# Batches 3 and 4 of a gated-linear-attention and mixer kernel: q and k transposed by 24 transfers that ScalarE issues

## The chip, the cores and the metric

The kernel runs on one core of one Trainium2 chip. The metric is device time in microseconds (us), the median of several runs; lower is better. A profile of one execution goes with it. Engines are named as in the profile: PE is TensorE's matmul (PEld its weight loads), DVE is VectorE, ACT is ScalarE, POOL is GpSimd, SP is SyncE, which only issues transfers. SPq is SP's own instruction queue.

## The reference: what is computed

q, k, v and alpha have the shape 4 batches x 8 heads x 768 positions x 48. Two parts follow each other. The first is a recurrence over positions with a state of 48 x 48 per head; the second is a mixer over the positions and channels of what the first gives (384 channels, a low-rank position mixing of rank 32, and a two-layer MLP of width 1536).

```python
for t in range(S):
    state = alpha[:, :, t, :, None] * state + np.einsum('bhd,bhe->bhde', k[:, :, t], v[:, :, t])
    y[:, :, t] = np.einsum('bhd,bhde->bhe', q[:, :, t], state)
...
h = xt @ U @ V                       # xt: x with positions last
u = x + h.transpose(0, 2, 1)
ch = np.maximum(u @ w_ch1, 0.0) @ w_ch2
return (u + ch).astype(np.float32)
```

Inputs and the output are 32-bit floats; the kernel works in bfloat16 with 32-bit accumulation.

## The kernel before, in words

**Chunks.** The recurrence is done in chunks of 128 positions, six per batch (c = 0 to 5). Batches are numbered from 0, so the third and fourth batch are 2 and 3. In batch 0 all chunks, and in batch 1 the first four, go through `stage_pair`, which works on halves of 64 positions; the other two of batch 1 and all of batches 2 and 3 go through `stage_gla`, which the change touches. For one chunk `stage_gla` does this, in names used below:

- ACT takes the logarithm of alpha into `lt` (line 525); a matmul with a triangle of ones sums it up over the chunk (lines 532 and 534); ACT takes the exponentials of plus and minus that sum, `aa` and `ai` (lines 542, 543), and of the totals, `tot` (line 545).
- POOL (or DVE) multiplies: `rk` = k times `ai`, `rq` = q times `aa` (line 552, both). v is cast to `rv`.
- `rk` and `rq` are transposed into `kT` and `qT` (tiles kt and qt): the head dimension comes to the partitions. In batches 0 to 2 PE does it, four 128 x 128 transposes each against an identity (`f_tr`, line 565), and DVE or ACT copies the result out of PSUM (`f_ev`). In batch 3 SP issues one transposing transfer for each (line 576), SBUF to SBUF, 128 x 512 bfloat16.
- Scores are matmuls of kT and qT (`f_sc`, line 590, eight per chunk), masked by DVE into `pm` (line 600). The state is a matmul of rk and rv (line 613), added to the state before it on DVE (line 640) and scaled on POOL or DVE (line 624). The chunk's output is the matmuls of line 652 (from the state) and of line 657 (from pm and rv), copied to `xb`.

The pools of these tiles are small: three of kT, four of qT, three of rq and four of rk, so a transpose into a kT also waits for the scores of the chunk that had that tile before.

**Mixer.** `stage_mix` does the low-rank part and adds it to x (lines 672, 702 and 703), and transposes the sum with PE (line 723). `mlp1` is 24 entries per batch of three 384-wide matmuls each (line 754), each followed by a ReLU out of PSUM on ACT (line 764) or DVE (line 766). `mlp2` is, per chunk, twelve 384-wide matmuls in three groups of four (line 780), then an addition on DVE (line 786) and one or two output transfers by SP (lines 789 and 791).

**Order.** Nothing is ordered by loops at run time. Every operation is entered in a plan with a list of the engines it may use and an estimate of its cost in ns. The estimates serve an offline search only. What runs is the string TABLE: three characters an entry, two of them the operation's number (base 64) and the third the engine, P, A, D, G or S. An entry that begins with ++ issues as many filler matmuls (line 259) as its third character's number says. SLOTS gives, in order of first use, which buffer of its pool each tile takes. So each engine runs its entries in the order of TABLE, and an instruction at the head of an engine's queue that waits for a semaphore holds all that follow it on that engine.

Batches overlap in the order: the chunk work of batch b + 1 lies between the `mlp1` and `mlp2` matmuls of batch b, so that PE has work while other engines prepare chunks. PSUM has eight banks, shared by all of this. Inputs go into 36 buffers (`io`), so a load also waits for a buffer.

In the order before, the engines hold, of the entries that the change's steps touch:

| | before |
|---|---|
| transposes of batches 2 and 3 | batch 2: 12 groups on PE with 12 copies out (6 ACT, 6 DVE); batch 3: 12 transfers on SP |
| ReLU entries on ACT, batches 0 to 3 | 17, 13, 12, 12 |
| ReLU entries on DVE, batches 0 to 3 | 7, 11, 12, 12 |
| filler matmuls | 9, near the start |

Of the kernel before, what the change touches and what calls it, by code (L numbers as in the profile page):

```python
# [15 lines left out]
TABLE = """
++EA8SCcACePChABQSETAEVPA+SCgACjDClPBASCzAC1PCfA++BA9SCiDCkPBISCnADjAA-SCdGCrPCsDBDSC3AC4ACmACoPCpD++DBBSC2AC5DDlPDnAABS
AFGAGPCqDBCSC6GC0GC8PC+DEWAEXADmABMSD8ABLSDkGC7P++BC9DDCPDDDCtPC-PDADDBDBKSDqGCuDBESDKAEYAD+PDEPDFDDoAAHDDMPDOADNABFSDQD
BJSDpGDPABHSDLGBRSEZGBSSBYSCvPCwPCxDDZPDGPDsPDuABUSDHPDJADrPDtDBGSDRGDSPEaDDyPBNSBTSEUGDzPD0DEBAD-ADIAECGBOSEAAEDGDvPDwD
DUAEcPEbPEdDDaPDbDD1PD2DAJPEeAEfPEhDEgDG2AGfAGhPDTPDVDDcPDdDBPSD9GCyAAKABVSGiAGlGBgSAOSAPGBWSGjAGmGBcSAgSAhGAASADGBXSG4P  # L20
ALGAMSGgGANGBoSAQSARGBZSAiSGkAG7AG5AG8GDxDBaSG6AG9GASSBbSAeSEiPEjPBkSBiSAWSDWPDXDBdSD3PD4PAUSBfSBeSEEPEGAD5PD6AAaSAcSBhS
A2SAmSAYSEFPEHAEkDDePElPEmPELPDfPBlSBqSEnPEpAHmADYDDgPEoADhADiDEMPBjSBpSEOPENDEIPEKDEJDGnPHoPAoSBmSAqSAkSEPPGoPGqDHNAHPP
EQPESDERDGpAGrPGsDGtDD7AHpAHQAEqPErPEwPE5PE2PHqAHrAGuPHRAGvDGwDEsAEtPE6PE7AExPE3PE4DE8PFBPFCDEuPEyAE9PE+AAwSB0SAuSAySEzP
FJPFFPFGDFKDE0PIVAEvAE1AGyPE-PFlPFmAG+PFADFjPFkAFHPFIDBnSG-PHBDFnPFoDGxGFPPAsSACSA6SBrSHSAHAAHCPG3GHFPHGDHHDHEDGzPA4SAfA
AjGFdPFeAG1DA0SF3PF1PF2DHDDF4DH-AHIGG0AF5PIBPIFAFhPFiAIXPHJPF6AIEAFfPFgAIYAFQAHTDBsSBtSFNPAXGHtGHvPAVGATGFVPFtPFWAIDAHxD
FODFTPFUAHUGHWPIZAHKPHLAFuDHOGHcPHYAHdDFrPAdGHsGFDPFEDHVPHXDHuPHeGHfDICAHwDFsAAnAFLPFMAHMAHgDHiPFRPFSAHZPHaDHbDB8SBvSB3S
HyPB4SBwSHzDIGDH0DAZGAbGFZPH6PFaAFXPFYAA3AFxPHhPFvPFwAIbGIdPIfDFbPFcAHjPHlAHkDHnGH1PH2DH3DIaGFzPF0AH4DB2SIIPIKDIHGIJPIcP
IeDH7PFpPILAFqDH8PH9DH+AIgPH5DFyDIMPIODCASINDIhDArGApGAIGAlGGTPF7PGZPK0AK2PGBPAvGBuSAzAIAAIPPIRDIQDAtAITPK4AAxGGUPGaPF8P
IiDIWAISGIjPA7AK5AGCPK3AIUDAEGK6AIkAIlPA1AImAA5GGDPF9PGEDI1PI2DIpPIqDInPGNPIvPIwDItPIoDIuDGVPGWDIzPI0DF+DBySBxSGASF-SGOP
KLAKNPKPAKTGKOAKSGBzSIrPIsAIxPIyDGPPI3PI4DGbPGcDKfAJNPJdPI9PJHPKhPJOALeAJIDJFPJeAJGDI+AKiAI5PKjALJALzAI6DJTPJUDI7PI8AKQA  # L30
LgPJVPLjAKRALiAKlALkAJLPJMDJRPLhAJJPJDPJnPJKDJjPKUPB1SJWAJSAJPPI-PJAAKkAJoDJkDGQDJBPJCAJZPCCSJaAKWAK7DK9PK-DGFSKMGKbPKcD
JhPJiAKgGKmGKnGKvPL1PL2AJEAB-SJXPLLPLNALMAJQDLPAKwDK8DJfPJgDKoPKpPKrAB+SKqAGYSK+PLOAGdSB6SGXSB9SLlGLADJYDKxDL3AL5GCESJlP
JmAJbPGeSB5SLQGCBSL4GKVPKXDJvPK1AKsPKtDCFSJcAB7SCISCRSCMSLBPKYPLDDJwPNlANnPNpAL7PL9ANrANoALCDGGSGHPKuDLEPLFDKZDJxPJyDLGD
KyPKzAGIPL6PL8DLHPGJPKaDCQSNqALIDLnPLpDGKDGSSCUSJ0SCDSCGSCHSLSPLRGLTPKBPGRSLmGLoPLKALZPLqDKCPLaDLrPLtDLsDLfALUALVALWPLYD
L+PKDPKEDJ7POKAOMPLbGLxPNsGNuSNtGNvSOdAOfPOhAOjAOgAOOAL-DMADLXDJ8PJpPLuPLvDLwDJ9PJ+DJqPKdPKeDN3AN5PN6AOPAOwAOiAL0GMBPMCD
N7ALyAONAJ1PNmGNzPGLSJzSN0DCJSN+GCOSOSGCSSOlGGMSCYSCTSCWSKFSCKSOkGOmSCLSJrPLcPLdAJ2PN9ANwPNxDMDPJsDNyDMEAKGPCVSMTPOnSMLP
MNPMODOQAN8AMFPKHPMHPMRPJ3PN1PMMDMPPMQAMIDN4GMGDMJPMKDOyPO2AOzAO1AKIPMjPMtPMuAMUDMSDMVPMWDMkAPDAKJDMlPMbPMnPMoAMxPPFPPGA
J4DMmDMvPMfPMwDMgDMcAOASNDPNEAM5PM6DMXPMyDMZPMaDN2DMdPO0AO4DM3PCNSMrPMsDMpPMqACZSMeDCPSN-GOBSCaSO6SNBPOoPMYDOqDM7PNCAM1P
MhPM9PM2AMiDOpDO3GO5SCXSOUSORGOTSM-POeGOLGOFPOGDOHDPHAM4ANMPNHPOYPMzPM+DM8DOZDOrPNRPNFPNGAOaGNAAOsDNIPOuPOvDNNPOCPODDO7P
PIGPKSPJGPLSJ6SCbSM0ANJPNbPNSPJ5SOxGO+POEDOIPOJAJtSO9DOtDJuSNOPO8DPBPO-DPADPCAOVPOWDOXDNcPPEANWPPMPPODPNDNTPNUDNVSObPOcA  # L40
NgPPPPPQANhPPRPPSANiPNKDKKSNLSKASPTPPUDPZPPbPPcDPVPPWDNXPPaDPfPPgDNdPPhPPiDPXPPYAPdPPeDNYPPjPNjDP7PP8APpPNeDPqDPrPPkDNPD
NQSPlPPxPPsDP1PPtPPuDPyDQDPQHPQNPQOAQBPQCDQLPQMAQIAPnPPoAP-PQAAPzPP9PPmDP0AQRPQTPQUDQSDNZDNaSNkSQEDQPPQVPQQAP+AJ-SNfSQFP
QGAQJPPvPPwDQuPQaPP5PP6AQKAP3PP4DQzPQfPQWPQ0PP2DQXPQYDQZSQ1PQ2DQ3SQgPQbPQkPQcPQdDQeSQhPQvPQiDQjSQlPQwPQpPQxDQySQmPQnDQoS
QqPQrPQsDQtS
"""
SLOTS = """
AAAABBBCAACDCDAEAEFAAGAFGAHBBAACAIBBECFJBBDBCAAKBLCABHCBDABMCNCCHDBBBOCPDAQDRASTEDAAGCCUBFCVACBDWXEGCBABYCCFBCAHDBCDFDHD
AABAGAZAaBDbcdABefgEhBijABDACCDBACEFFGIJDHBHGALKNCCMPQORSBBBEDFCGTVCUXHABFCGCWYZaDECBFBGBAABAEDHCCCGACAAAABCAcbdeGDHAECB
AHADfGDCBghjBAAFCDHBBBGiCBADHCCFDEGHACADEDCECABAEBBCDECABAEBGDCCDBBBBFGEDCBFGACJIADBHGEDBAACGDCBAACABLGACDFCCADBGDFBCCAC
HBEFHADABABCDAAGBABBEDGFBBECNKCFCBBAPDBBADAECDBABBHCEBCABCBDHCCDEBBCFECDQHBCECSBBGCCBBAECAECCMDGBABBCBAHBRAFVUDAAAAOEBTA  # L50
XCHDFDADAYZWabGCEHBBBAACDBCGACBDACDAGdECDcefgACFBBDAHBBGEABBAACBFDAHAECGBCABCCBAACABFABCDBACBAEFABCDHAjChCiBADIBABJGCDFC
HBAGCDDHBCEAFBHCBAEDCHAADCDFAHDGAACFAHACFAHCAEHADEFBCPAFBAADHFCDCKBBBACEHBCBGFEBAHCDBBEDHBAECABDQBADHCDEABADADHEABADAEDB
BCAEFDCFDAECAFBDDEBABFDCGEDBEDBGAEBDBEDAGHCEACBADCDEBA
"""


# [81 lines left out]
def kernel(  # L138
# [383 lines left out]
    def stage_gla(b, c, sprev, xb):  # L522
# [51 lines left out]
        if (b, c) in QUEUE_T:
            for dst, src in ((kT, rk), (qT, rq)):
                P.add({"SP": 900.0}, lambda e, dst=dst, src=src: nc.sync.dma_start_transpose(dst(), src().rearrange("t h w -> t (h w)")), r=[src], w=[dst], kind="T")
# [268 lines left out]
```

## Time and profile before

| | |
|---|---|
| median of three runs | 165.25 us (163.98 to 166.45) |
| the profiled execution's own time | 166.14 us |
| its span, first to last instruction | 164.4 us |
| mean granted TensorE clock | 0.990 |
| line 754 (mlp1 matmuls), 288 | 52.0 us busy |
| line 780 (mlp2 matmuls), 300 | 54.2 us busy |
| line 565 (PE transposes of rk and rq), 64 | 5.8 us busy (219 ns each, pipelined) |
| line 576 (transposing transfers on SP), 12 | 2.5 us from issue to landing for kt, 3.2 for qt |
| loads of q, k, v, alpha, 96 of 192 KB | 3.6 to 3.9 us from issue to landing |

Busy time is the time in which an engine had at least one instruction under way; matmuls overlap in the pipeline, so the mean duration of one is longer than what it adds. What one matmul adds is read from the chain, where a group's time is the step to the next group. Transfers are issued by a sequencer (SPq rows) and moved by 16 shared DMA engines, whose mean busy share is given by stretch. "Idle before, releaser" names what an engine last waited for.

### The profile page before, as it was taken

Reading aid. Unit: us, or ns where it says so; the run is one execution under the profiler, and the core shown is the slowest. Engines: PE = TensorE matmul, PEld = TensorE weight load, DVE = VectorE, ACT = ScalarE, POOL = GpSimd, SP = SyncE. Lnnn points to the kernel's source line nnn. Section 1 sums busy time; section 2 is a strip of 40 time slices with the busy share of each in tenths; the row PEclk is TensorE's granted clock in tenths of the full one; section 3 lists DMA queues with packets and bytes.
Section 4 is the critical chain, followed back from the end, with each engine's and each line's share of the span. In section 5 each row is a group of like instructions: output and inputs, shape, how many; then the busy total and the mean of one; then the engine's idle time right before and its main releaser. Section 6 shows DMA issues by size and latency. Waiting matters only on the chain.

```text
span 164.4 us, 4606 instructions
## 1 busy us (share of the span) xinstructions
PE 153.7 (94%) x1767; PEld 101.2 (62%) x1767; DVE 118.6 (72%) x254; ACT 86.5 (53%) x223; POOL 60.7 (37%) x99
## 2 busy tenths in 40 slices
PE   5875999999998999999999979999999999999992
...
DMA  5999999999999999899998759889653550105053
GB/s 136 291 312 305 273 264 222 311 260 287 238 273 290 231 212 197 172 220 208 214 196 174 145 114 227 193 160 183 114 106 68 136 175 4 48 0 168 5 186 102
DMA packets 94758, 30.49 MB, mean 185 GB/s; under 512 B 88432, under 2 KB 94704, under 8 KB 94736
## 3 DMA queue, kind: packets, MB, share of 16 engines
...
q14 instruction: 8, 0.07, 0.1%
...
## 4 chain that ended last, share of the span: by engine, by line
PE 76%; SPq 11%; DVE 4%; DMA 3%; POOL 2%; issue 1%; ACT 1%; DVEq 0%; POOLq 0%
PE ps L780 27%; PE ps L754 27%; SPq L325 10%; PE ps L702 2%; PE ps L590 2%; PE ps L565 2%; PE ps L723 2%; PE ps L402 2%; DMA io<-in_moe_w_ch_dram 2%; DVE pm L437 2%; PE ps L657 1%; PE ps L509 1%; DMA out_dram<-ou 1%; PE ps L532 1%; PE ps L652 1%
## 5 line engine op out<-in xcount | busy, mean ns | idle before, releaser
L780 PE MATMUL ps<-w_sb,h1t 128*128 128x384 bf16 (+2 forms) x300 | 54.2, 320 | 0.9 <-ACT tot L545 0.9
L754 PE MATMUL ps<-uT,w_sb 128*128 128x384 bf16 x288 | 52.0, 326 | 0.0
L764 ACT ACTIVATE h1t<-ps 128x384 bf16<-128x384 f32 x54 | 25.5, 501 | 25.0 <-PE ps L754 24.8
L780 PEld LDWEIGHTS <-h1t 128*128 128x128 bf16 x300 | 26.7, 97 | 16.3 <-issue 1.9
L754 PEld LDWEIGHTS <-w_sb 128*128 128x128 bf16 x288 | 26.6, 98 | 15.5
L766 DVE TENSOR_SCALAR h1t<-ps 128x384 bf16<-128x384 f32 x42 | 22.2, 553 | 12.3 <-PE ps L754 11.6
L600 DVE TENSOR_TENSOR pm<-ps,maskc 128x512 bf16<-128x512 f32 x28 | 18.1, 684 | 3.4 <-PE ps L590 2.5
L786 DVE TENSOR_TENSOR ou<-ub,ps 128x384 f32<-128x384 bf16 (+2 forms) x25 | 13.2, 534 | 9.1 <-PE ps L780 8.2
L552 POOL TENSOR_TENSOR rq<-io,aa 128x384 bf16<-128x384 f32 x12 | 10.9, 916 | 12.3 <-DMA io<-in_q_dram 7.7
L552 POOL TENSOR_TENSOR rk<-io,ai 128x384 bf16<-128x384 f32 x12 | 10.9, 916 | 11.3 <-DMA io<-in_k_dram 5.8
L703 DVE TENSOR_TENSOR ub<-xb,ps 128x384 bf16<-128x384 bf16 x24 | 12.0, 550 | 2.3 <-PE ps L702 2.1
L437 DVE TENSOR_TENSOR pm<-ps,maskp 128x512 bf16<-128x512 f32 x20 | 13.1, 683 | 0.6 <-PE ps L426 0.2
L270 POOL CAST rv<-io 128x384 bf16<-128x384 f32 x18 | 9.1, 511 | 11.9 <-DMA io<-in_v_dram 11.9
L266 ACT CAST xb<-ps 128x192 bf16<-128x192 f32 (+1 forms) x21 | 8.0, 388 | 8.0 <-PE ps L657 7.3
L543 ACT ACTIVATE aa<-ps 128x384 bf16<-128x384 f32 x14 | 7.0, 497 | 8.5 <-PE ps L534 8.5
L270 POOL CAST w_sb<-io 128x384 bf16<-128x384 f32 x17 | 8.8, 533 | 0.9 <-DMA io<-in_moe_w_ch_dram 0.9
L385 POOL TENSOR_TENSOR rq<-io,aa 128x384 bf16<-128x384 f32 x8 | 7.6, 950 | 3.3 <-DMA io<-in_q_dram 1.9
L624 POOL TENSOR_TENSOR st<-sm,tot 128x384 bf16<-128x384 f32 x3 | 2.5, 830 | 15.3 <-DVE sm L640 15.3
L542 ACT ACTIVATE ai<-ps 128x384 bf16<-128x384 f32 x14 | 7.0, 503 | 1.8 <-PE ps L534 1.7
L379 ACT ACTIVATE aa<-ps 128x384 bf16<-128x384 f32 x10 | 5.0, 506 | 5.4 <-PE ps L371 5.4
L525 ACT ACTIVATE lt<-io 128x384 bf16<-128x384 f32 x14 | 7.2, 532 | 0.0
L385 DVE TENSOR_TENSOR rk<-io,ai 128x384 bf16<-128x384 f32 x4 | 6.2, 1554 | 1.1 <-ACT ai L378 1.1
...
## 6 DMA issues: line engine op xcount, KB each, us to landing
...
```

The source lines that it names most:

```text
L270: nc.gpsimd.tensor_copy(dst, src)
L325: lambda e: nc.sync.dma_start(t().rearrange("p (h j) d -> p h (j d)", j=2), src[b, hs, sl, :].rearrange("h (p j) d -> p h (j d)", j=2)),
L385: eng.tensor_tensor(jh(dst()[:, :, 0:D]), raw(a), jh(x()), op=ALU.mult)
L437: nc.vector.tensor_tensor(dst, s2, maskp.to_broadcast([C, 2, 2, C]), op=ALU.mult)
L552: eng.tensor_tensor(dst()[:, :, 0:D], a(), x(), op=ALU.mult)
L600: nc.vector.tensor_tensor(pm()[:, :, par, :], s2, maskc.to_broadcast([C, HP, C]), op=ALU.mult)
L703: P.add({"DVE": 465}, lambda e, c=c, hb=hb: nc.vector.tensor_tensor(ub()[:, c, :], xb()[:, c, :], hb()[:, 0:DM], op=ALU.add), r=[hb] + xk( ...
L754: nc.tensor.matmul(hb()[:, 0:TW], lhsT=w1_sb[:, ct, jt * 128 : (jt + 1) * 128], rhs=u_half(uT, ct, tt, b in QUEUE_U), start=(ct == 0), sto ...
L764: nc.scalar.activation(dst, hb()[:, 0:TW], AF.Relu)
L766: nc.vector.tensor_scalar_max(dst, hb()[:, 0:TW], 0.0)
L780: nc.tensor.matmul(hb()[:, 0 : hi - lo], lhsT=h1()[:, jt, c * C : (c + 1) * C], rhs=w2_sb[:, jt, lo:hi], start=(jt == 0), stop=(jt == NJ - 1),
L786: P.add({"DVE": 468}, lambda e, hb=hb, lo=lo, hi=hi: nc.vector.tensor_tensor(ou()[:, lo:hi], ub()[:, c, lo:hi], hb()[:, 0 : hi - lo], op=A ...
```

## The change

Batch 2's chunks too are transposed by transfers, and all 24 transfers of batches 2 and 3 are issued by ScalarE on its own queue instead of by SP. TABLE and SLOTS are replaced as a whole. All else is the same, the estimates of other operations included.

```diff
     PAIRS = {0: 3, 1: 2, 2: 0, 3: 0}
-    QUEUE_T = tuple((3, c) for c in range(6))
+    QUEUE_T = tuple((b, c) for b in (2, 3) for c in range(6))
     LAST, CUT = 3, 240
...
         if (b, c) in QUEUE_T:
             for dst, src in ((kT, rk), (qT, rq)):
-                P.add({"SP": 900.0}, lambda e, dst=dst, src=src: nc.sync.dma_start_transpose(dst(), src().rearrange("t h w -> t (h w)")), r=[src], w=[dst], kind="T")
+                P.add({"ACT": 1200.0}, lambda e, dst=dst, src=src: nc.scalar.dma_start_transpose(dst(), src().rearrange("t h w -> t (h w)")), r=[src], w=[dst], kind="T")
         else:
```

The new TABLE has 1068 operations where the old one has 1080. Read entry by entry, with the operations numbered in the order in which the code enters them:

| | before | after |
|---|---|---|
| transposing transfers | 12 on SP (batch 3) | 24 on ACT (12 each for batches 2 and 3) |
| transposes on PE, batch 2 | 12 groups, 12 copies out | none |
| ReLU entries on ACT, batches 0 to 3 | 17, 13, 12, 12 | 14, 3, 7, 13 |
| ReLU entries on DVE, batches 0 to 3 | 7, 11, 12, 12 | 10, 21, 17, 11 |
| products and casts on POOL, batches 2 and 3 | 29 | 33 |
| filler matmuls | 9 | 2 |

In the new order ACT issues batch 2's transfers among the mlp1 and mlp2 matmuls of batch 1, chunks in the order 0, 2, 1, 5, 3, 4, and batch 3's among those of batch 2, chunks in the order 0, 3, 1, 4, 2, 5.

More of the change, by code (lines that the diff above doesn't have):

```diff
@@ L21 @@
[L21 to L35, printed above, removed]
@@ new lines @@
+CtPClPBESDKADMPEYABRSEZDDFDCnACoPBISC9DC-PCuDCqDCpDDGPDBDBMSDPADjAD8AD+PDOADNADlPDoADADDmAABSAFGAGPDnAAJPAKDBGSDRGBJSDpG
+BHSDLGBFSDQDBKSDqDEbPEdAAHAAIGBSSEaGBLSDkGBYSCvPCwPCxACyADrPDtADZPDTPDVDDHPDaPDbDBUSD-ABNSECGBPSDIADsPDuADJADSPDUDDcPDdD
+EcPEeDG2AGfAEBADvPDxDDwDDyPDzPD0DDWPDXDEAABOSEDGBTSEUGGhPGjAD9ABWSGmGGiABgSBcSBVSGkABXSGgGAASG4PG6AELPADGBaSG9GAgSAhGAeS
+AfGAiSDYDD4PD1PD2DBZSASSD3PEEPEGDAjGEMPENDD5PG5AG8GAMSANGG7AAOSEfPEgDEhDDfPD7AD6ABiSEFPAPGAQSBbSARGAUSAVGBeSBdSEHADePElP
+EiPAWSAXGBhSHmABoSDgPDhAAaSBjSAcSHNADiABkSEjPAYSBfSBqSAoSBmSEkDEIPEKDGlDBlSHoPHqAHtGHrABpSAqSAmSAuSAkSAsSBnSAwSEJDAySA0S
@@ new lines @@
+A6SB0SEmPGoPGqAEPPBrSEnPEoAA2SA4SACSEOPHpAEpAHPPHRAHQAHSAHUGGnPGpDEQPESDERDGuPGvDEqPGrPGtDGsDGwDAdGBuSAbGErPEsABwSE8PE2P
+EzPEwPE9PE+ABsSE3PE4DGxDExPFDPEtPB8SB4SFJPEyAE0PE1AEuPEvDE5PFBPFCDFHPFEDG-PHBAE6PE7AGyPFIDFhPFiAG+PATAHAAFfPFgDE-PFFPFKD
+FADF3PF4AF1PF2DHCPHDDFGDB1SBtSBvSFdPHEDF5PFlPFmDFeDFnPGzPG3AHFPF6AHsDHGDHTDHHDHIGFNPFOAFLPFoAFjPFkDFMAFrPFsAG0AIVAFpPFVP
+HvPHuPHxDHwAHWPHYDFTPFUAFqDG1DIXPIYAHyPHzDH0DFRPIZAFtPFuDH-AHVPHJPHXDIBPIFAICAFSAAZGFzPF0DFxPFyDIEAIDAFvPFwAFWDHKPHLAHMA
+HOGHcPHdDHeDHnGH1PH2DHfDHZPHbDHaDIbGIdPFZPFaAIfAFPPFQAIHGIJPFbPFcAIGGIIPIKDAnAFXPFYAArAILDIaGIcPIeDHhPHiPH3GH4DH5DH6PH7P
@@ new lines @@
+HjPHkAH8PH+AAxAApGIMPINDIODIgPIhDAlGF7PGNPGBPGZPHlDIiDHgGIAGITPIPPIQDIRDISDAvGAzAAtAGaPGTPGCPGUPA7GA1AH9AKwAKyPKzAK1AIUA
+IWGIjPA5GIkDF8PA3GGDPGEDGGSALGAEGIlPImAK2AF9PF+DF-SGASK0AIpPIqDIvPKdAKLABxSItPIuDIwDGVPIzPCASKfPKhAKgAKjAKNPCESKPAKTGInP
+IoDB2SBzSBySGbPKiAGWDCBSCCSB3SB+SIxPIyAKOAI0DKSGI1PI2DGOPIrPIsDGcDGPPB6SB5SI3PI4DB7SB9SGYSGFSJJPJLPI5PI6DJRPJjPJSDJKDJnP
+JoDJlPJmDGXSCGSI9PGQDGRSCFSJMDJfPCMSGSSCQSB-SCISCDSKQALWALYPCHSGeSK3GLDAKVAKUAJkAGdSK5ALaAKRAI+AJPPJQAKWPKXDJHPJIDJFPJGD
+JgDJDPLpALrPLcAJNPJODKYDJXPJYDGHPKMGKZPKaDLFPJTPJUDJBPI7PJCDI8DLbAKkGKmAJhPJiDJEDJbPK4GI-PJADJZPJaDKeGKrPKsDLsAK6AJcDLZA
@@ new lines @@
+GIPJvPKbPKcDLtAKlGKnAKoPKpDKqDLuGNZALGALHAK7PK8DK9DKtDJwPGJPNbPJpPKuPKvDKxGK+PK-DJxPJyDJ0SJzSJVPJWDCUSCRSGKDGMSGLSLwACVS
+CSSCKSCYSLJAJdPJeDCJSCLSCWSCNSCOSCTSLvGLxALIACaSCPSLBPLyPLzDL0DKBPJqPLKGLMALeGLgACZSLADLCDLEGLRPKCPLSDJ7PKDPKEDKFSLLGLNA
+LOPLdGLfALhPLiDLjDNcANgGNeANdAN+ANiANfANhGNjAJ8PLXGLkPJ1PLTGLnPLlDLmGORALoALqAOAPOBAODAOTPOXAOWAOUAOYGJrPL1PLPDLQDLUPOVA
+OZGL2DOCAJ2PNkPLVDL3PNlDNmDNaAJ9PJ+DJ-SKASCXSL4AL-PMBPMCDMADL7PKGPOEAMHPL5PL6DMFPKHPL8DJsDJuSNrANpPNqDOkAMDPMEDL9PL+AJ3P
+NnPNtPNvANuANxAOmPOnAMGDMRPMVPMWANoDJ4DJ6SJtSMTPCbSOrGMhPMIDMJPMKDMUDMXPMSAMbPMcDMYDOaAMnPNyGMiAMPPOoANwAObAOqAO3AOpAMQA
@@ new lines @@
+MfPNzDMoDN1AMtPMuDMrPMNPMODMgDMpPMLPMqDMMDMZPO5PO7AMdPO6AMaAM3PM4DMvPMwDMsDMeDMlPOcPOeDM5PM6DMmDMxPN0AOFGOsGNsGN5POSGN6D
+N7DMjPMkDNAPOtAOGGOuAMyAOHAM7POIAJ5SN-GOMPONDNBPMzPM0DOdDNCPOfPNFPNDDNESOOGOiPOjAOgDM8PO9GO-AOvPOxDOwDN2PN3DN4DNPPKIPOJP
+OKDKJDO8GO+ANGPM9PNQPN8PN9AOlGOhDOyPOzDO0GNHPPAPNUPO1PO2AOLDOPPOQAPBDM1PO4GPCDPDPPEANVPM2APFPPGANWPNXDPPPPHPPIDPJPPNPNRP
+NKPPKDPTPPQDPVPNLPPLPPODPRPNMPPMAPWDPUDPXPPYAPSDPbPPpPPdPPqAQDPNSDQEDPeAQHPPfPQFPQGAPcAM+DM-SPzPP0DPgDQIDP-PPhPQADPxPPZP
+PyDPiDP7PPvPPrPNTSPlPPmAP5PNIDP6APjPPkDP3PPaAP4DNYSNJSKKSQBPQCAPnPQTPP1PPtPNNDPwAPsANOSPoAP2DQJPP9PP+AQiPQKPP8DQUPPuAQLP
@@ L45 @@
+QMDQNSQnPQjPQOPQVPQWDQXSQoPQPPQYPQpPQqDQrSQkPQlDQmSQQPQRDQSSQZPQdPQaPQbDQcSQePQfPQgDQhS
 """
 SLOTS = """
[L47 to L50, printed above, removed]
@@ new lines @@
+AECBJFEDGAFACHBAGCACDFBAGBAHOEFCBADDGBACBFCEFBABCDFAAABGEADFCACBBGHBEDCDFABGCADABEEFBACBABGADHCEDDACBCAGACHCBDAEBBGFACAE
+BBGHADFCDBAAHAHBBBGBEABGHDKCCCCGIAAHLMQCPRNSEBACHCDUVFWYDEHBCBFHTCBaDXcdZeBCFbBABBCABHACGECBBDHGEDDAHAGDAAAGBDACCBAABFDC
+BCCBABDCCCCGABDBAECAAGfgCBhiBjBADECJFHADAOHCFCGCABBGCBEBABCCCFACHEBADCBBBAAAGDDHAAADECAGBBBHACABCFHGBCDKACFCGHEAFACCABAC
+GBCBADABGFABCBLCDFEGAFABABCADCDGECFGACBBBDFGCACDFCDAEEABDBABBCADADGAEFBBAGBCBECAAFBGCECDABABCFAACHAFEBCCHFBAEHACFAHCEFAC
+HEFBCCGEFBCDFHCEGDHFBBHFCBHFCAGDACHBEDCAGB
```

19 lines of the change are left out of this document (3 added, 16 removed).

## The prediction

> **What bounds the kernel now.** I read the page first (busy shares, slices, chain), then the table of stretches, then the rows of the transposes that already run as transfers, then the chain of waits around them.
>
> ```profile
> PE 153.7 (94%) x1767; PEld 101.2 (62%) x1767; DVE 118.6 (72%) x254; ACT 86.5 (53%) x223; POOL 60.7 (37%) x99
> ...
> DMA  5999999999999999899998759889653550105053
> ...
> PE 76%; SPq 11%; DVE 4%; DMA 3%; POOL 2%; issue 1%; ACT 1%; DVEq 0%; POOLq 0%
> ```
>
> TensorE is busy 94% of the span and is 76% of the chain that ended last; SP's issue of the first loads is the other part.
>
> ```profile
> 34.00:54.00 20.00, 19.41 (x289) 12.86 (x288) 17.29 (x39) 15.11 (x41) 14.22 (x24) 1.00 1.02 271
> ...
> 64.00:82.00 18.00, 18.00 (x163) 12.10 (x162) 12.99 (x27) 13.54 (x37) 5.41 (x7) 1.00 0.96 202
> 82.00:92.00 10.00, 10.00 (x145) 7.14 (x144) 9.02 (x19) 6.68 (x17) 5.37 (x7) 1.00 0.91 184
> 92.00:100.00 8.00, 7.09 (x92) 4.92 (x91) 6.35 (x12) 4.17 (x12) 2.77 (x5) 1.00 0.63 131
> 100.00:115.00 15.00, 15.00 (x137) 9.39 (x134) 11.14 (x23) 6.50 (x18) 7.49 (x10) 1.00 0.92 191
> 115.00:135.00 20.00, 19.91 (x215) 12.44 (x214) 15.05 (x29) 6.26 (x14) 3.09 (x5) 1.00 0.54 123
> ```
>
> Columns: stretch, its length, then busy time of TensorE, weight loads, VectorE, ScalarE, GpSimd, then granted clock, DMA share, GB/s. From 34 us on TensorE idles only 0.59 + 0.91 + 0.09 = 1.6 us before the tail. So a microsecond taken off TensorE there is a microsecond off the end, if nothing else becomes late. VectorE (9.02 of 10 us at 82 to 92) is next, DMA is near full until 92 us, ScalarE has room.
>
> ```profile
> L576 SPq DMA_TRANSPOSE kt<-rk x6: 1191/1218/1308, 92.8 to 123.8; - x6
> ...
> DMA to landing us min/median/max: 2.4/2.5/2.6
> ```
>
> ```profile
> L576 SPq DMA_TRANSPOSE qt<-rq x6: 1188/1388/1719, 94.3 to 125.1; - x6
> ```
>
> ```profile
> 94.58 0.85 SPq L576
> 95.44 0.05 issue
> 95.49 1.94 DMA out_dram<-ou
> 97.44 0.25 ACT tot L545
> ```
>
> A transpose holds its issuing sequencer 1.19 to 1.72 us; ten that stand alone in SP's rows have a mean of 1.36. It lands 2.4 to 4.1 us after its issue begins. The last fence is the chain: the one TensorE stall of 0.91 us runs through SP's transposes.
>
> **TensorE's part, removed.** Batch 2 loses 12 groups of four transposes. The chain's rows give 0.22 us for a group ("PE ps L565 x4"), 0.67 us for three. 12 x 0.22 = 2.64 us, all in stretches where TensorE is 100% busy (64 to 92 us): on the path. The 12 evictions go too: on ScalarE 6 x 0.6 = 3.6 us, on VectorE 6 x 0.42 = 2.5 us, both beside TensorE, worth nothing by themselves.
>
> **ScalarE's part, added.** Read entry by entry, the new table gives ScalarE 24 transposes; at 1.36 us that is 33 us of its queue. In return ReLU evictions move: ScalarE 54 to 37, VectorE 42 to 59 (in batch 1's first matmul, ScalarE 13 to 3). Everything behind a transpose on ScalarE waits for its issue, and the score matmul (line 590) waits for its landing. I walk the two crowded stretches, with ScalarE's step of 0.39 us for a 384-wide activation (69.79 to 70.18 in its rows), 0.15 for a small one, and TensorE's groups of 0.49 (first matmul) and 0.65 (second).
> Stretch A, from the ReLU after batch 1's twelfth first-matmul entry to the scores of batch 3 chunk 0: ScalarE has 11 transposes, 11 activations (4.4 us), 6 small ones (0.9) and the last landing (2.5 - 1.25 = 1.25): 6.55 + 11x. TensorE has 23.5 us of work ahead of those scores. With x = 1.36: 21.5, slack 2.0. For the scores of batch 2 chunk 4: 5.05 + 9x = 17.3 against 18.9, slack 1.6.
> Stretch B, batch 3: 2.85 + 5x = 9.7 against 10.8, slack 1.1. So at the measured price ScalarE hides it all; the slack is gone at x of about 1.54 (A) and 1.59 (B), and beyond it each 0.1 us costs 1.1 + 0.5 us. Where x on ScalarE is not SP's, the bounds are 1.19 and, from SP's slowest transpose, 1.72; a plain load on SP stretched to 2.47 us at 54.42 as the farthest row. I take 1.36, the same instruction on the nearest queue: 0 us.
> GpSimd's products feed these transposes; its list for stretch A (eleven of 0.92, four casts of 0.51) is 12.2 us in 23.5: hidden.
>
> **VectorE's part, added.** In batch 1's first matmul TensorE has 11.6 us from the first to the last but two entries; VectorE has 19 ReLUs at a step of 0.47 (three in 1.53 us at 70.25), two masks of 0.605 and three other 0.47: 11.5 us. Its densest stretch now, 84 to 92 us, ran 7.50 of 8 us (94%). 11.5 / 0.94 = 12.2, so TensorE waits 0.6 us for PSUM. Bounds: 0 (steps back to back) and 24 x 0.1 = 2.4 us (half the 0.18 to 0.20 us gaps of rows where VectorE waited for TensorE, paid each time). I take 0.6.
>
> **DMA, SP and the start.** Twelve transposes more: at 125 to 127 us two of them make up a share of 0.64 of 2 us, so 0.64 us each, 7.7 us in all, where the share is 0.91 to 0.96. Cover: at 80 us of TensorE work the new table has issued 121 of 123 loads, the old one 108; 13 loads at about 1 us are 13 us of lead. Gone, it would cost up to 7.7. SP loses 12 transposes (16 us), so loads behind them are no longer held; that may give back the 0.91 us, or nothing if another wait takes its place: I take 0. The start: 9 filler matmuls become 2, the loads of batch 0 end at the 27th load in both tables, and first-layer weights follow at the 35th to 37th (30th to 38th before): 0, cover being the loads themselves. The granted clock was 0.50 at 16 to 18 us after an idle 12 to 14 us, so fewer fillers could keep it there: the 2.4 us of TensorE work between 9.6 and 15 us at half clock is +2.4 at most; below, TensorE is busy only 2.43 of the 5 us from 10 to 15 us, and a luckier order could take up to those 2.6 us back.
> By the Trainium skill, TensorE: Matmul & The Clock Gate, Part 1, the clock follows about 3.4 us of activity rather than a number of matmuls; by that, seven fillers of 0.2 us spread over the start hardly decide it, and the sum would stay as it is.
>
> **Sum.** -2.64 + 0.6 = -2.0 us. The profiled execution took 166.14 us (span 164.4, 1.74 around it) and would take 164.1; it lies 0.9 above the median of 165.25, so the median goes to 163.2.
>
> **Rivals.**
> 1. More than the sum: the VectorE wait does not come, and the 1.6 us of stalls goes with SP's transposes. For it: the only long stall's chain runs through line 576. Against: all orders are new, and new orders have their own gaps. 165.25 - 2.64 - 1.6 = 161.0.
> 2. Slower: ScalarE's transpose costs more than its slack. Place: stretches A and B. Stall 11(x - 1.54) + 5(x - 1.59). At SP's slowest 1.72 it is 2.6 us and the gain is gone (165.25 with no VectorE wait, 165.9 with it); at 1.93 it is slower by 2%; at 2.0, 7.1 us and 169.7. For it: in stretch A SP issues 15 loads back to back beside about six transposes, and two of SP's own took 1.66 and 1.72 among loads. Against: ten had a mean of 1.36 in a share of up to 1.10.
> 2b. A milder form: each of six transposes waits for one load's issue on SP (0.54 us): 3.2 us against 1.6 to 2.0 of slack, 1.4 us of stall, 164.6.
> The Trainium skill, Perfetto Trace Analysis, "DMA Instruction — HWDGE", says that the two issuing sequencers share one descriptor generator, locked for one instruction at a time, and that the reported duration holds the wait for the lock; by it 2b is what happens. No trace here has two issuing engines at once.
> 3. VectorE is the bound in batch 1's first matmul: 2.4 instead of 0.6, 165.0. For it: 99% of TensorE's time by steps. Against: 82 to 92 us, crowded too, cost TensorE nothing.
> 4. The start is longer by 2.4 us: 165.6.
>
> **How the numbers follow.** Two per cent, 3.3 us, is about what a measurement of this kernel can tell from no change: under 161.95 is faster, over 168.55 slower. Forecast 0.38 (162.2 to 164.2); rival 1 0.24 (160.2 to 161.9, nearly all faster); 2b 0.14; 2 0.14, most of it past 168 only if x passes 1.93 (0.09); 3 0.06; 4 0.04. Faster 0.26, counting 0.03 from the forecast's own lower edge and less for rival 1's upper one; slower 0.10; same 0.64. Range: 160.6 leaves out about 0.07 below, 167.0 about 0.12 above.
>
> **What would show it.** Line 565 falls from 64 matmuls to 16. ScalarE's rows carry 24 transposes: their duration against 1.54 decides rival 2, and TensorE's idle time before line 590 prices it. VectorE near 95% busy with TensorE idle before line 754 in batch 1's first matmul shows the 0.6 or rival 3. TensorE idle at 92 to 100 us gone: rival 1. The first line 754 matmul later than 34 us: rival 4. Batch 3's GpSimd products waiting for loads would show that the 13 loads of lead are no cover. I am wrong if TensorE is not near 100% busy from 34 us on.

## The result, and the profile after

| | before | after |
|---|---|---|
| median | 164.64 us (163.98 to 166.45) | 169.39 us (168.94 to 169.69) |
| profiled execution, its span | 166.14, 164.4 us | 168.94, 167.1 us |

The ratio of after to before is 1.03, with a 95% interval of 1.0237 to 1.0362: slower by 3%, and outside the range given (160.6 to 167.0). Some executions of a kernel take a per cent or two longer than others; the profiles of runs 1, 9, 14, 15 and 17 below are of such executions, and of those only waits, issues and landings are read.

The page of the changed kernel: busy shares, DMA slices (each a fortieth of the span, in tenths), and the shares of the chain that ended last.

```profile
PE 149.5 (89%) x1712; PEld 97.9 (59%) x1712; DVE 118.5 (71%) x262; ACT 76.3 (46%) x200; POOL 64.4 (39%) x102
...
DMA  5999989999998999999998999999999200321115
...
PE 62%; DMA 14%; SPq 14%; DVE 3%; POOL 3%; issue 2%; ACT 1%; POOLq 0%; ACTq 0%; DVEq 0%
```

TensorE has less to do (153.7 us fell to 149.5), and yet is no longer busy enough: it is 62% of the chain where it was 76%, and landings of transfers are 14% where they were 3%. The table of stretches of the same kernel (columns as in the prediction) says where:

```profile
34.00:54.00 20.00, 19.86 (x299) 13.38 (x295) 18.64 (x40) 13.51 (x35) 13.01 (x21) 1.00 1.04 273
...
64.00:82.00 18.00, 16.03 (x144) 10.05 (x143) 14.27 (x29) 6.29 (x17) 7.70 (x10) 1.00 1.38 185
82.00:92.00 10.00, 8.91 (x94) 5.72 (x92) 7.99 (x16) 1.29 (x4) 3.98 (x5) 1.00 0.97 189
92.00:100.00 8.00, 3.79 (x38) 2.33 (x35) 3.51 (x6) 1.42 (x4) 3.91 (x5) 0.79 1.26 186
100.00:115.00 15.00, 14.69 (x154) 9.52 (x153) 11.39 (x23) 9.86 (x28) 3.65 (x4) 1.00 1.01 198
115.00:135.00 20.00, 20.00 (x219) 12.55 (x219) 15.86 (x30) 4.18 (x10) 8.46 (x12) 1.00 0.92 176
```

From 64 to 100 us TensorE idles 1.97 + 1.09 + 4.21 = 7.3 us; before it idled 0.9. ScalarE, which got the transposes, computes for only 1.29 of 10 us at 82 to 92; issues and waits are not in that figure, and from 82.6 to 90.9 us its queue does nothing but wait at four transposes and issue them. No engine is short of computing time there. What everybody waits for is read from the chain of waits in order of time (start, duration, what), two pieces of it:

```profile
70.34 4.79 DMA io<-in_q_dram
75.14 0.07 issue
75.21 0.92 POOL rq L551
76.13 0.02 issue
76.15 4.79 DMA qt<-rq
80.94 0.14 issue
81.08 0.62 PE ps L589 x16
...
90.00 3.47 DMA io<-in_k_dram
...
93.64 0.92 POOL rk L551
94.56 0.67 SPq L331
...
95.32 5.77 DMA io<-in_v_dram
...
101.11 0.52 ACT rv L265
101.63 0.04 issue
101.67 0.36 PE ps L656 x8
```

Both are loads that come too late, and take long to land. The first piece is a load, a product of GpSimd, a transpose of 4.79 us, then the scores; the second is two loads, and at its end a cast by ScalarE and the output matmuls. The rows of ScalarE's transposes, then what SP's own queue waited for (total, times, longest), and ScalarE's longest wait:

```profile
L575 ACTq DMA_TRANSPOSE qt<-rq x12: 1206/1234/1686, 63.6 to 125.6; - x12
L575 ACTq DMA_TRANSPOSE kt<-rk x12: 1204/1224/1389, 65.3 to 127.1; - x12
...
DMA to landing us min/median/max: 2.5/4.4/5.7
```

```profile
SPq L331 <- DMA qt<-rq: 4.9, 5, 1.7
...
SPq L788 <- DMA kt<-rk: 3.6, 1, 3.6
...
SPq L331 <- DMA kt<-rk: 2.0, 1, 2.0
...
SPq L788 <- DMA qt<-rq: 0.7, 2, 0.5
```

```profile
ACT ai L541 <- DMA qt<-rq: 8.4, 1, 8.4
```

The issue costs what was forecast, and a little less: a mean of 1.28 us for 1.36. The landing does not: a median of 4.4 us for 2.5. And SP, which only loads and stores, waits 11.2 us for ScalarE's transposes; before, it had no such wait. This comes from how the program is built: the queued transfers of SP and ScalarE take eight completion semaphores in turn, and each waits for the one eight places before it in the merged program. The longest of these waits stands just ahead of the second late piece: a transpose of kt issued at 85.48 landed 3.9 us later, an output transfer of SP waited 3.6 us for it, and the load of k at 90.00 stood behind that transfer. Counted in SP's rows, 102 loads had been issued by 88 us before, and 96 after; the loads that were issued at 64 to 92 us took a median of 4.1 to 5.9 us to land (by input), before 3.4 to 3.8. So the loads are six behind just where TensorE runs dry.

### The profile page after: what moved, and what is told of

Same layout as the page of the kernel before. It is cut to its first block, busy times and chain, and to the rows that moved or that the text cites. A ratio compares the mean times of both kernels' runs of the same rounds, so it can differ in the third digit from the quotient of the medians.

```text
span 167.1 us, 4547 instructions
## 1 busy us (share of the span) xinstructions
PE 149.5 (89%) x1712; PEld 97.9 (59%) x1712; DVE 118.5 (71%) x262; ACT 76.3 (46%) x200; POOL 64.4 (39%) x102
## 3 DMA queue, kind: packets, MB, share of 16 engines
q10 hardware_dynamic: 13056, 3.15, 12.8%
## 4 chain that ended last, share of the span: by engine, by line
PE 62%; DMA 14%; SPq 14%; DVE 3%; POOL 3%; issue 2%; ACT 1%; POOLq 0%; ACTq 0%; DVEq 0%
PE ps L779 24%; PE ps L753 23%; SPq L324 12%; DMA io<-in_v_dram 3%; DMA io<-in_moe_w_ch_dram 3%; DMA io<-in_q_dram 3%; DMA qt<-rq 3%; DMA io<-in_k_dram 2%; PE ps L701 2%; PE ps L722 2%; DVE h1t L765 2%; PE ps L589 2%; PE ps L656 1%; PE ps L531 1%; PE ps L651 1%
## 5 line engine op out<-in xcount | busy, mean ns | idle before, releaser
L753 PE MATMUL ps<-uT,w_sb 128*128 128x384 bf16 x288 | 51.2, 326 | 0.0
L765 DVE TENSOR_SCALAR h1t<-ps 128x384 bf16<-128x384 f32 x59 | 30.1, 552 | 8.6 <-PE ps L753 6.6
L763 ACT ACTIVATE h1t<-ps 128x384 bf16<-128x384 f32 x37 | 17.1, 494 | 17.4 <-PE ps L753 14.5
L551 POOL TENSOR_TENSOR rk<-io,ai 128x384 bf16<-128x384 f32 x14 | 12.8, 923 | 22.5 <-DMA io<-in_k_dram 20.5
L551 POOL TENSOR_TENSOR rq<-io,aa 128x384 bf16<-128x384 f32 x13 | 11.9, 914 | 12.5 <-DMA io<-in_q_dram 7.0
L269 POOL CAST rv<-io 128x384 bf16<-128x384 f32 x19 | 10.3, 543 | 12.2 <-DMA io<-in_v_dram 12.1
L384 POOL TENSOR_TENSOR rq<-io,aa 128x384 bf16<-128x384 f32 x9 | 8.4, 945 | 2.8 <-DMA io<-in_q_dram 2.8
L589 PE MATMUL ps<-qt,kt 48*128 48x128 bf16 x112 | 5.2, 218 | 4.6 <-DMA kt<-rk 2.3
L542 ACT ACTIVATE aa<-ps 128x384 bf16<-128x384 f32 x14 | 6.8, 497 | 5.6 <-PE ps L533 5.6
L267 DVE CAST xb<-ps 128x384 bf16<-128x384 f32 (+1 forms) x11 | 5.1, 477 | 4.3 <-PE ps L656 4.3
L544 ACT ACTIVATE tot<-ps,off 128x4 f32<-128x4 f32 x22 | 5.7, 274 | 5.3 <-issue 3.0
```

Source lines behind the costliest of these rows:

```text
L269: nc.gpsimd.tensor_copy(dst, src)
L551: eng.tensor_tensor(dst()[:, :, 0:D], a(), x(), op=ALU.mult)
L589: nc.tensor.matmul(sc[par]()[:, p * C : (p + 1) * C], lhsT=kT()[o : o + D, p, :], rhs=qT()[o : o + D, p, :], start=(p == 0), stop=(p == HP ...
L753: nc.tensor.matmul(hb()[:, 0:TW], lhsT=w1_sb[:, ct, jt * 128 : (jt + 1) * 128], rhs=u_half(uT, ct, tt, b in QUEUE_U), start=(ct == 0), sto ...
L763: nc.scalar.activation(dst, hb()[:, 0:TW], AF.Relu)
L765: nc.vector.tensor_scalar_max(dst, hb()[:, 0:TW], 0.0)
```

## The experiments

Ratios are to the kernel before in the same job, with 95% intervals. Where two jobs are compared, differences of medians can be half a microsecond to a microsecond off, because the kernel before had medians from 164.6 to 167.2 us; the ratios are the safer figure. The theories changed on the way and are named in each expectation: D (the DMA engines' time that twelve more transposes take), S (ScalarE's queue stands behind transposes that wait for products), O (the new orders themselves), W (SP's waits for ScalarE's transposes), N (the number of transfers on two queues).

**1 and 2. Easier loads.** The 56 loads of batches 2 and 3 read the same bytes in runs of 384 bytes instead of 192 (other positions' data, so the result is of other inputs), in the changed kernel and in the one before.

```diff
-src[b, :, sl, :].rearrange("h t d -> t h d")
+src[b, hs, sl2, :].rearrange("h (p j) d -> p h (j d)", j=2)   # batches 2 and 3
```

> The changed kernel, but the 56 loads of q, k, v and alpha in batches 2 and 3 that are made of 192-byte runs read runs of 384 bytes instead (half of the heads for 256 positions: other data, the same bytes and tiles, half as many packets). ScalarE's queue, the transposes, the orders and all waits are the same. Theory D (the DMA engines were nearly full until 92 us, and 12 more transposes push the loads of batch 2 back): the 6 us of new TensorE idle time between 64 and 102 us goes, about 162 to 164 us. Theory S (ScalarE's queue holds work behind transposes that wait): little changes, 168 us or more. Theory O (the new order itself is bad, with SP's loads behind its output transfers): 167 us or more.

> The kernel before, with the same longer runs in the loads of batches 2 and 3 (other data, the same bytes). TensorE idles only 1.6 us after 34 us there, so whatever the theory: 163 to 165 us. Beside the changed kernel with the same loads it gives what the change is worth where DMA is not the limit: 2.6 us if theory D holds.

Measured: 164.15 us for the changed kernel, ratio 0.9837 (0.9718 to 0.9956), with a wide spread of 161.4 to 168.0; 164.31 for the one before, 0.9981 (0.9939 to 1.0023). Easier loads take back the whole loss of the change, though by how much is known only roughly, and give the kernel before nothing. So the loads hold TensorE up only after the change. That does not yet say what burdens them: the longer runs also made a load's issue on SP cheaper (a mean of 0.50 us at 64 to 92 us, 0.98 in the changed kernel), so this run eases SP's queue as well as the DMA engines.

**3 and 4. The transfers at the old orders.** Batch 3's twelve transposes issued by ScalarE at their old places; and that with batch 2's twelve as well, in the place of TensorE's.

```diff
-P.add({"SP": 900.0}, ... nc.sync.dma_start_transpose(...))
+P.add({"ACT": 900.0}, ... nc.scalar.dma_start_transpose(...))
```

> The kernel before and its order; only batch 3's 12 transposes are issued by ScalarE instead of SP, at the same places of the order. Theory D: the DMA work is the same, so 163.5 to 166 us. Theory S: ScalarE now waits for products and holds what follows it; 166 us or more. SP's loads no longer wait behind transposes in either.

> The kernel before and its order, but with all 24 transposes on ScalarE: batch 2's stand where the copies out of PSUM stood, and its TensorE transposes are gone. Theory D: TensorE waits for loads as in the changed kernel, 167 to 171 us. Theory O: without the new order there is no loss, 162 to 164 us. Theory S: a loss too, 167 us or more, with ScalarE's queue on the chain rather than loads.

Measured: 182.47 us, 1.1045 (1.0956 to 1.1133), and 195.21, 1.1809 (1.1721 to 1.1898). TensorE's longest wait in the first is 4.8 us for ScalarE's `lt` (line 525), which stood behind transposes. At an order that was not made for it ScalarE's queue costs much, so theory S lives on; the new orders are needed for the change, and whether they remove all of it is open.

**5 and 6. The merge written out.** The build merges the engines' instruction lists into one program, and the order of that merge decides which transfer gets which semaphore. This is the changed kernel with the engines' instructions merged in the table's order, and with SP's entries moved in it so that few of its transfers stand eight places behind a transpose.

> The changed kernel with one difference in how its program is put together: the instructions of all engines are merged in the order of the table (every engine's own order stays as it is), where the build otherwise merges them by its own estimate. What that changes: the queued transfers of all engines take eight completion semaphores in turn, so that each waits for the transfer eight places before it in the merged order to land. In both merges 19 of SP's transfers stand eight places behind a transpose of ScalarE's. It is the control for the next run. Theory W (SP's queue is held by these waits, 11 us of them in the changed kernel's trace): between 168 and 172 us, SP's waits on transposes in sum 8 to 14 us. Theory D (the loss is the DMA engines' time that 12 more transposes take) and theory S (the loss is ScalarE's queue, where work stands behind a transpose that waits): 169.4 us, as the changed kernel.

> As the run before, but SP's transfers stand elsewhere between the other engines' instructions of the merged order, each queue's own order unchanged, so that the transposes of ScalarE come in threes with five of SP's transfers between: then a transpose stands eight places behind a transpose, and only 3 of SP's transfers stand behind one (19 before), and 3 transposes behind one of SP's (19 before). Bytes, transfers, queues and orders are the changed kernel's. Theory W: SP's waits on transposes fall from about 11 us to under 3 us, the loads of the fourth batch come earlier, and the time falls to 163 to 166.5 us. Theory D: the bytes and transposes are the same, so 168.5 to 170.5 us. Theory S: ScalarE's queue is the same, 168.5 to 170.5 us.

Measured: 945 and 954 us. In the first, TensorE is busy 31% and its ReLUs on VectorE wait 101.8 us for it: this merge adds waits of its own between all engines and swamps the question. Both tell nothing of W.

**7. All 24 on SP.** The changed orders, `nc.sync` for `nc.scalar`.

> The changed kernel's orders with all 24 transposes issued by SP at the same places of the table instead of by ScalarE. No wait between two queues is left, but SP now stands at a transpose until GpSimd's product is there, and pays 24 issues of 1.2 to 1.4 us. Theory S: ScalarE's wait of 8.4 us and its 24 issues of 1.22 us are gone, so 165 to 167 us. Theory D: same bytes and transposes, 169 to 170 us. Theory W: the loads behind a transpose wait in SP's own order, all of them instead of every eighth, and SP has 29 us more to issue: 171 us or more.

Measured: 212.23 us, 1.2855 (1.2743 to 1.2968); the scores wait 23.7 us for kt and 20.4 for qt. SP stands at each transpose until its product is there, and the loads behind it stand too. Moving the transposes off SP is right for these orders.

**8. Half the bytes.** Each transpose moves 256 of its 512 columns (the other half of the tile keeps old values).

```diff
-nc.scalar.dma_start_transpose(dst(), src()...)
+nc.scalar.dma_start_transpose(dst()[:, 0:2, :], src()[:, 0:4, :]...)
```

> The changed kernel with each of the 24 transposes moving only half of the columns (128 x 256 instead of 128 x 512; the other half of the transposed tiles keeps old values, so this leaves work out). Places, queue and waits stay. Theory D: the DMA engines' time of the 12 more transposes halves, from 12 x 0.89 = 10.7 us to 5.3 us, and the loss of 4.8 us falls by half or more: 164.5 to 167 us. Theory W: what holds SP is when a transpose can start, at the end of GpSimd's product, and only its landing of 4.4 us gets shorter, by about 1 us: 167.5 to 169 us. Theory S: an issue falls from 1.22 us to about 0.7 us, 12 us of ScalarE's time over the kernel, but the waiting transposes hold the queue as before: 168 to 169.5 us.

Measured: 170.36 us, 1.0328 (1.0226 to 1.0429): as the changed kernel. From its profile, the queue of ScalarE's transfers (packets, MB, share of the 16 engines) and the transposes' rows:

```profile
q10 hardware_dynamic: 6912, 1.58, 4.9%
```

```profile
L575 ACTq DMA_TRANSPOSE qt<-rq x12: 1183/1243/2321, 65.6 to 128.3; - x12
L575 ACTq DMA_TRANSPOSE kt<-rk x12: 1182/1186/1375, 69.0 to 129.6; - x12
...
DMA to landing us min/median/max: 2.3/4.2/6.6
```

The share fell from 12.8% of 167 us to 4.9% of 168: 13 us of packet time are gone from the 16 engines and nothing came back. Theory D, priced by that time as in the prediction, falls. What did not change with the size is the issue (1.19 to 1.24 us) and the landing (4.2).

**9. Another merge.** All orders and transfers unchanged; only the interleaving of the engines in the program differs, and so which transfer waits for which.

> The changed kernel, every engine's and queue's order and every transfer unchanged. Only the order in which the instructions of different engines are merged into one program is another (by the build's timed estimate), and with it which transfer gets which of the eight completion semaphores that all queued transfers take in turn: a transfer waits for the one that had its semaphore before. In the changed kernel 13 of SP's loads and 5 of its output transfers wait in this way for a transpose of ScalarE's; in this merge 6 loads and 11 output transfers do. Theory W (SP's loads are late because they wait for transposes that wait for products that wait for loads): SP's waits of loads on transposes halve from about 7 us, and the time falls to 165 to 168 us. Theories D (the DMA engines' time) and S (ScalarE's queue): 169.4 us, between 168.5 and 170.5.

Measured: 177.64 us, 1.0677 (1.0599 to 1.0755), where W had said 165 to 168. SP's waits for transposes did go, to 1.5 us, and it issued 28 transfers at 64 to 92 us instead of 22. But now TensorE waited for the transposes:

```profile
PE ps L589 <- DMA qt<-rq: 5.0, 2, 4.6
PE ps L589 <- DMA kt<-rk: 2.9, 1, 2.9
```

The first transpose was issued at 68.8 us instead of 63.6. W, as SP's waits alone, falls. A merge that changes only which transfer waits for which moved the time by 6 us by the ratios (8 by the medians), so these waits matter in both directions.

**10 and 11. Transposes that wait for nothing.** They read a constant tile of zeros; behind each ScalarE copies one column, of the zeros (10) or of the product (11, so that its queue is held as in the changed kernel).

```diff
-nc.scalar.dma_start_transpose(dst(), src()...)
+[nc.scalar.dma_start_transpose(dst(), filler), nc.scalar.copy(scr, filler[:, 0:1])]          # 10
+[nc.scalar.dma_start_transpose(dst(), filler), nc.scalar.copy(scr, src()[:, 0, 0:1])]        # 11
```

> The changed kernel with the 24 transposes reading a tile of zeros that is there from the start, and not GpSimd's products (which are still computed, but nothing of the third and fourth batch's q and k goes into the scores). At each place ScalarE also copies one column of the zeros, so that its work is that of the next run. No transpose waits for a product, so ScalarE's queue is not held and SP's loads find their semaphore free; the transfers, their bytes, their issues and their places are the changed kernel's. Theory D: the DMA engines' work is unchanged, so 168 to 170 us. Theories W and S: the waits are gone, 160 to 164 us, with TensorE near 100% busy from 34 us on.

> As the run before, but the column that ScalarE copies behind each transpose is one of the product that the transpose read in the changed kernel, so ScalarE stands there until the product is there, as it did at the transpose; the transposes read zeros and the scores of the third and fourth batch are left without q and k. A transpose now starts when the product before it is there, one product earlier than in the changed kernel. Theory S (ScalarE's queue is what costs): 167 to 170 us, as the changed kernel, and most of the difference to the run before comes back. Theory W (SP's waits for late transposes): transposes land earlier by about one product (1 us of GpSimd and its load), SP's waits shrink but don't vanish: 162 to 166 us. Theory D: 168 to 170 us.

Measured: 174.89 us, 1.0567 (1.0508 to 1.0627), and 176.78, 1.0627 (1.0533 to 1.0721). No theory saw that coming: for run 10 those that blame waits said 160 to 164 and D said 168 to 170, and without any wait for a product it is slower than the changed kernel. Part of this lies at the start, before any transpose: the first mlp1 matmul began at 33.5 and 33.7 us, in the changed kernel at 30.8. Why is not known. Between the two, holding ScalarE makes no difference that the intervals tell apart. Loads at 64 to 92 us landed after 4.2 to 6.0 us here.

**12 to 14. Transposes left out.** None (the transposed tiles are zeros, so q and k of batches 2 and 3 don't reach the scores); a one-column copy by ScalarE in each place, which waits for the product and lets the scores wait for it; and that for the q products with the k products transposed by transfers.

```diff
-nc.scalar.dma_start_transpose(dst(), src()...)
+None                                                                  # 12
+nc.scalar.copy(dst()[:, 0, 0:1], src()[:, 0, 0:1])                    # 13
+nc.scalar.dma_start_transpose(...) if src is rk else nc.scalar.copy(...)   # 14
```

> The changed kernel with all 24 transposes left out: the transposed tiles are zeros from the start, and q and k of the third and fourth batch don't go into the scores. All other work, all orders and the loads stay, and nothing takes the transposes' place on ScalarE. Theory O (the new orders themselves place the loads too late): 167 us or more. Theory N (what costs is that ScalarE's 24 transfers stand among SP's: they share eight completion semaphores in turn, each queue waits for the other's, and an issue on one lengthens one on the other, whatever a transfer moves): 158 to 162 us. Theory S (ScalarE's queue is held by transposes that wait for products): 158 to 162 us too.

> As the run before, but at the place of each transpose ScalarE copies one column of the product into the transposed tile. So ScalarE's queue stands at each place until GpSimd's product is there, and TensorE's scores wait for it, as with the transposes, but no transfer is issued; the scores of the third and fourth batch use that one column only. Theory S: 166 to 169 us, most of the loss of the change. Theory N: 159 to 163 us, within 1.5 us of the run before. Theory O: 167 us or more.

> As the run before for the 12 q products (one column copied), while the 12 k products are transposed by transfers as in the changed kernel: half of the transposes. Theory N: between the run before and the changed kernel, 163 to 166.5 us, SP's waits on transposes and the lengthening of its issues both about halved. Theory S: as the run before, whatever its time. Theory O: 167 us or more.

Measured: 159.27 us, 0.9687 (0.9616 to 0.9758); 159.88, 0.9717 (0.9652 to 0.9783); 167.26, 1.0126 (1.0029 to 1.0224). The stretches of the kernel without transposes:

```profile
64.00:82.00 18.00, 18.00 (x160) 11.35 (x159) 16.13 (x32) 6.89 (x21) 10.79 (x14) 1.00 0.88 182
82.00:92.00 10.00, 10.00 (x125) 6.70 (x124) 9.64 (x19) 2.77 (x8) 5.34 (x7) 1.00 0.97 205
92.00:100.00 8.00, 8.00 (x104) 5.32 (x102) 7.26 (x15) 5.37 (x16) 1.01 (x2) 1.00 0.80 170
```

TensorE idles nowhere from 64 to 100 us. This settles two theories: the new orders are good (O falls), and ScalarE's queue held for the products costs 0.6 us (S falls at these orders). 169.4 - 159.3 = 10.1 us go with the transposing transfers. Half of them cost 7.4 of the 9.5 us over the run with only the copies (6.7 of 9.6 by the ratios; its four runs spread from 165.4 to 168.2), so the loss is not in proportion to their number.

**15 to 17. Twelve small transfers in the kernel before.** 128 rows of 128 bytes, from a constant tile to a spare one, behind each copy of batch 2's transposes, issued by ScalarE, GpSimd or SP.

```diff
 def f_ev(e, dst, tb):
     copy(e, dst(), ...)
+    if b == 2:
+        nc.scalar.dma_start(spares[-1], filler[:, 0:64])    # 16: nc.gpsimd, 17: nc.sync
```

> The kernel before with 12 small plain transfers more (128 rows of 128 bytes, 16 KB each, from a constant tile to a spare one that nobody reads), issued by ScalarE behind its or VectorE's copies of the third batch's transposes, where the change puts its transfers. They wait for no data; 0.2 MB in all is 0.6% of what the kernel moves. Theory N: they stand among SP's transfers in the rotation of eight, so SP's loads and ScalarE's queue wait for each other: 166 to 170 us. Theories D, S and O: 164.5 to 166 us, the kernel before.

> The kernel before with the same 12 small transfers (16 KB each, constant tile to spare tile) at the same places of the table, issued by GpSimd on its own queue, which takes other completion semaphores than the rotation of eight that SP's and ScalarE's share. If the shared rotation makes the cost of the run with ScalarE (168.0 us): 164.5 to 166 us. If the DMA engines or merely twelve more transfers do: 167 to 169 us. GpSimd pays about 1 us for each issue by an estimate from its 0.9 us products, in time of which it has some left, so up to 1 us of that could be GpSimd's.

> The same 12 small transfers issued by SP at the same places of the table. They take places in the rotation of eight, but all in one queue, which works through them in its own order, so no queue waits for another; SP pays 12 issues more of some 0.5 us, 6 us at 78 to 91 us, where it issued for 23.0 us of 28. If the waits between two queues make the cost: 164.5 to 166.5 us. If SP's time or the number in flight does: 167 to 170 us.

Measured: 168.02 us, 1.0179 (1.0086 to 1.0271), on ScalarE; 165.59, 1.0026 (0.9987 to 1.0064), on GpSimd; 170.73, 1.0311 (1.025 to 1.0372), on SP. Their rows in these three kernels, in that order:

```profile
L576 ACTq DMA_DIRECT2D spare<-filler x12: 472/510/619, 78.3 to 91.3; - x12
```

```profile
L576 POOL DMA_DIRECT2D spare<-filler x12: 534/538/709, 69.3 to 88.9; - x12
```

```profile
L576 SPq DMA_DIRECT2D spare<-filler x12: 587/647/1500, 72.6 to 100.8; - x12
```

The same 0.2 MB costs nothing on GpSimd's queue, which has other semaphores and no loads, and 1.8 to 3.1% on the two that share the rotation. On SP the 12 issues of 0.65 us are 7.8 us taken from the loads, enough to account for it. So SP's queue has little to spare in the kernel before already, and what slows it shows in the time.

**18. Small plain transfers in the transposes' places.** The changed kernel with each transpose replaced by a plain transfer of 64 columns of its product (the scores use these alone): same places, same waits for products, same rotation.

```diff
-nc.scalar.dma_start_transpose(dst(), src()...)
+nc.scalar.dma_start(dst()[:, 0, 0:64], src()[:, 0, 0:64])
```

> The changed kernel with each of the 24 transposes replaced by a plain transfer of 64 columns of the same product into the same transposed tile (16 KB for 128 KB, no transposing, an issue of 0.5 us for 1.2 us), issued by ScalarE at the same place; the scores of the third and fourth batch use these columns only. The waits for the products and the places in the rotation are the changed kernel's. If the number of transfers on two queues and their waits make the cost: 166 to 169.5 us. If the transposing itself (its 1.2 us of issue, its landing of 4.4 us) does: 160 to 163 us, near the runs without transposes (159.3 and 159.9).

Measured: 161.43 us, 0.9775 (0.9731 to 0.9818). Its transfers' rows:

```profile
L577 ACTq DMA_DIRECT2D qt<-rq x12: 472/473/565, 64.5 to 117.9; - x12
L577 ACTq DMA_DIRECT2D kt<-rk x12: 472/472/614, 65.8 to 118.7; - x12
...
DMA to landing us min/median/max: 1.7/2.9/4.7
```

Number, places and waits for products cost 161.4 - 159.3 = 2.1 us. The other 8.0 us up to 169.4 go with the transfer being a transpose of 128 KB and not a plain one of 16 KB (by the ratios 1.5 and 8.7 us). So N, too, is the smaller part of it at these orders. A plain transfer of 128 KB in the same places was not run; of the bytes only the step from 128 to 64 KB was tested (run 8).

The runs side by side, for the stretch of 64 to 92 us (loads: median from issue to landing by input, lowest to highest; last column: SP's waits for ScalarE's transfers, whole span):

| kernel | time | loads issued by 88 us | landing | SP's waits |
|---|---|---|---|---|
| before | 164.6 | 102 | 3.4 to 3.8 | 0 |
| orders, no transposes (12) | 159.3 | 102 | 3.6 to 3.9 | 0 |
| small plain transfers (18) | 161.4 | 101 | 3.3 to 4.0 | 5.9 |
| half the transposes (14) | 167.3 | 95 | 4.2 to 4.5 | 5.1 |
| changed | 169.4 | 96 | 4.1 to 5.9 | 11.2 |
| half the columns (8) | 170.4 | 96 | 3.2 to 5.2 | 12.3 |
| reading a constant (10) | 174.9 | 94 | 4.2 to 6.0 | 6.7 |

In this table every kernel with transposes on ScalarE has issued 94 to 96 loads by 88 us, and every one without has 101 or more. That is where the two kinds part. It does not rank them: the counts of the four with transposes lie within two loads, and their times 7.6 us apart. SP's waits don't rank them either: 5.1 us with half the transposes and 5.9 with the small transfers, 167.3 and 161.4 us.

## Why the prediction was wrong, point by point

**The step that failed** is the one on DMA and SP: "Gone, it would cost up to 7.7", taken as 0 because 13 loads of lead in the order were to cover it. The cover was not there in time. When TensorE had done 80 us of work, 102 of the 120 loads into `io` had been issued before the change and 97 after, and only 101 in run 12, which has the new order and no transpose to wait for. So the new order gives SP no lead at that point even when nothing disturbs it, and with the transposes it is four loads fewer still, with SP's waits for them and slower landings beside them. The loss that came, 7.3 us of idle TensorE at 64 to 100 us, is near the 7.7 named, but that is chance: the term was an engine time of 0.64 us a transpose (0.89 by the share after), and halving the columns gave nothing back. What the runs show in its place is a cost of 10.1 us for the 24 transfers at these orders, 2.1 of it for their number and waits and 8.0 for being large transposes.

**TensorE, -2.64 us**: not contradicted, but not measured alone. Line 565's 64 matmuls became 16, and without transposes the changed orders take 159.3 us, 5.4 less than before in the same job (164.7). That is more than the 2.64, and takes in the 12 transposes that SP loses, scores that wait for no transpose, and a start that is shorter, as follows.

**ScalarE, 0 us at 1.36 us a transpose**: the price held, by a mean of 1.28 us measured; so rival 2's price (over 1.54 us) did not occur, and that its 169.7 us at 2.0 lies near the result is chance. That a queue held for products costs little is shown by run 13 (0.6 us), but there without transposes. In the changed kernel ScalarE stood 8.4 us at one place: the walk through stretches A and B took a landing of 2.5 us where 4.4 came, and started from products that were to be there.

**VectorE, +0.6 us**: did not come. TensorE idled 0.0 us before line 753 in the changed kernel, and in run 12, where no load came late, it was busy for all of 64 to 82 us beside a VectorE busy for 16.13 of the 18.

**The start, 0**: some 1.5 us were gained. The first mlp1 matmul began at 30.8 us, 33.8 before. In the first 20 us the granted clock was 1.00, where it had been 0.91, in spite of 2 fillers for 9. Estimated from busy time to 34 us times clock, less 0.2 us a filler: 13.47 + 13.54 - 0.4 = 26.6 us of work done, against 14.46 x 0.91 + 13.72 - 1.8 = 25.1 before. The fear that fewer fillers keep the clock low did not come true.

**SP's loss of 12 transposes, 0**: there is no run for it alone; whatever it gave is in the 5.4 us.

**Rival 2b** (164.6) had two queues in each other's way, and named the wrong victim. On the mean ScalarE's transposes were not lengthened. The Trainium skill, Perfetto Trace Analysis, "DMA Instruction — HWDGE", says that the reported duration holds the wait for the shared generator's lock. The transposes' mean of 1.28 us, below the 1.36 on SP, shows no such wait; the longest, 1.69 us, may hold one. SP's loads at 64 to 130 us do in part: with a transpose's issue under way a load's issue took a mean of 0.95 us against 0.62 in run 8, 1.10 against 0.67 in run 10, but 0.91 against 0.82 in the changed kernel and 0.80 against 0.78 in run 14.
The Trainium skill, DMA: Bandwidth & Descriptors, "Issuing engines are not separate DMA queues", says that issuing on several engines saves the sequencer's time only, and that the transfers interleave on the same 16 engines. The runs agree: SP's time is what was bought here (run 7, with all 24 on SP, is 25% slower than the changed kernel), and the loads landed after 4.1 to 5.9 us beside the transposes where it had been 3.4 to 3.8.

**What stays open.** It is not known which property of a transpose does it: its issue of 1.2 us, its landing of 4.2 to 4.4 us, or the slower landing of the loads beside it. None of the three was changed alone. Run 8 rules out that the loss goes with the bytes between 256 and 512 columns, no more. Nor is it known why run 10, without waits for products, is slower than the changed kernel by 4.4 us (by the ratios); its start was 2.7 us later, and 9 of its 24 transposes had another of the eight semaphores. No run of the full computation on the given inputs beat the kernel before; TensorE's transposes at the new orders, the next thing to try, were not tried.
